# w_out with four consecutive rows on a partition, and layer one's weights taken from every fourth column of w_in

## The chip, the cores and the metric

The kernel runs on one core of one Trainium2 chip. The metric is the device time of one execution in microseconds (us). Executions of the kernel before agree within 0.6 us. Beside the times there is one execution recorded by the hardware profiler, with its own time; the rows and the trace that are read below come from that execution.

## What is computed

Sliding-window attention (a plain window of 32 keys for heads 0 to 3, a window of 32 keys at a distance of 4 for heads 4 to 7) is followed by a two-layer network with a SiLU between the layers. Only the second half is touched by the change:

```python
attn_out = _attn_ref(q, k, v)          # batch 8, heads 8, seq 576, head_dim 64
x = attn_out.transpose(0, 2, 1, 3).reshape(B * S, H * D)   # 4608 x 512
h = x @ w_in                           # w_in 512 x 2048
g = h * (1.0 / (1.0 + np.exp(-h)))
return (g @ w_out).astype(np.float32)  # w_out 2048 x 512
```

All inputs and the output are float32. The kernel works in float16 with float32 sums.

## The kernel before

**Batches and layers.** The outer loop runs over the 8 batches. For each batch, attention leaves its result transposed in `xT` (128 partitions, 4 pieces of 128 model columns, 576 positions). Layer one (`layer1`, from line 601; `layer1_part`, from line 618, for the two parts of batch 0) computes 16 groups `f` of 128 hidden units. A group takes 4 pieces `c` of the model dimension by 2 halves of the positions. Each of these 8 steps is a weight load of 128 x 128 elements of `w_in16` and a matmul over `xT` of 288 columns (line 606; 256 or 320 columns in batch 0, line 625). ScalarE then writes SiLU of the group to `gT[:, f, ...]` (lines 614 and 632). Layer two (`layer2_first` for batch 0, line 634; `layer2`, line 654) takes 128 positions of `gT[:, f]` as the stationary operand and `w_out16[:, f, :]`, 512 columns, as the moving one, and sums over the 16 groups (lines 642 and 666). `store` (lines 649 to 652) copies a sum to SBUF and sends it out on SP's queue.

**What a group is.** Hidden units are the sum index of layer two. Partition `p` of `gT[:, f]` and partition `p` of `w_out16[:, f]` must be the same hidden unit; which units make up a group is free, if all 2,048 are covered once.

**Loads of the weights.** Both weights are loaded in quarters of 512 hidden units, each with one DMA from GpSimd's queue, which also turns float32 into float16: `load_w_in(c)` at line 172 and `load_w_out(c)` at line 178. In `load_w_out` a partition gets four rows of a quarter, 128 rows apart.

**What sets the order.** Nothing is scheduled by a planner. Each engine runs its instructions in the order in which the program was written (`manual_schedule`, line 57), and the order around the layers is written by hand: `plan_of(b)` (line 690) gives, for each group `f` and for each step of layer two, the attention work of the next batches that is put in front of it. So TensorE's row is one fixed list in which stretches of layer-one matmuls, layer-two matmuls and small attention matmuls follow one another.

**GpSimd's queue.** It issues, in this order, the first batch's `q`, `k` and `v`, the four quarters of `w_in` (from 6.9 us), `load_qk(1)`, two quarters of `w_out`, `load_v(1)`, the other two quarters of `w_out` (lines 791 to 796), `load_qk(2)`, and the loads of the later batches. A DMA on this queue waits until the DMA eight places ahead of it has landed.

**PSUM.** The layers' sums `h` and `o` share two buffers (`big`); scores, transposes and attention results share four (`ps`).

Of the kernel before, what the change touches and what calls it, by code (L numbers as in the profile page):

```python
# [14 lines left out]
P = 128  # L15
# [12 lines left out]
def kernel(  # L28
# [44 lines left out]
    w_in16 = cpool.tile([P, MC, DFF], F16, name="w_in16")  # L73
# [96 lines left out]
    FC = DFF // 4  # L170

    def load_w_in(c):
# [2 lines left out]
            in_=moe_w_in[:, c * FC : (c + 1) * FC].rearrange("(c p) f -> p c f", p=P),  # L175
        )

    def load_w_out(c):
        nc.gpsimd.dma_start(
            out=w_out16[:, 4 * c : 4 * c + 4, :],  # L180
            in_=moe_w_out[c * FC : (c + 1) * FC, :].rearrange("(c p) m -> p c m", p=P),
        )


# [416 lines left out]
    def layer1(b, f):  # L601
        xT = state[b]["xT"]
        h = big.tile([P, 2, 512], F32, tag="big", name=f"h_{b}_{f}")
        for c in range(MC):
            for half in (0, 1):
                nc.tensor.matmul(  # L606
                    h[:, half, 0:HS],
                    w_in16[:, c, f * P : f * P + P],
                    xT[:, c, half * HS : half * HS + HS],
                    start=(c == 0),  # L610
                    stop=(c == MC - 1),
                )
        s0 = (b % 2) * S
        nc.scalar.activation(  # L614
            gT[:, f, s0 : s0 + S].rearrange("p (a c) -> p a c", a=2), h[:, :, 0:HS], AF.Silu
        )

    def layer1_part(f, part):

        xT = state[0]["xT"]  # L620
        c0, c1 = ((0, SA), (SA, S))[part]
        h = big.tile([P, 2, 512], F32, tag="big", name=f"h_0_{f}_{part}")
        for i in (0, 1):
            for c in range(MC):
                nc.tensor.matmul(  # L625
                    h[:, i, 0 : c1 - c0],
                    w_in16[:, c, (f + i) * P : (f + i + 1) * P],
                    xT[:, c, c0:c1],
                    start=(c == 0),
                    stop=(c == MC - 1),  # L630
                )
        nc.scalar.activation(gT[:, f : f + 2, c0:c1], h[:, :, 0 : c1 - c0], AF.Silu)  # L632
# [157 lines left out]

    load_qk(1)
    load_w_out(0)
    load_w_out(1)
    load_v(1)
    load_w_out(2)
    load_w_out(3)

# [28 lines left out]
    for b in range(B):  # L826
        plan = plan_of(b)
        if b == 0:
            for part in (0, 1):
                for f in range(0, NFF, 2):  # L830
                    plan(f - NFF * (1 - part))
                    plan(f - NFF * (1 - part) + 1)
                    layer1_part(f, part)
        else:
            for f in range(NFF):
                plan(f)
                layer1(b, f)
        if b == 0:
            layer2_first(plan)
        else:  # L840
            layer2(b, plan)
        for s in range(NFF, 3 * NFF):
            plan(s)
# [30 lines left out]
```

## Time and profile before

| | us |
|---|---|
| median of 3 runs | 332.45 |
| lowest, highest | 332.21, 332.79 |
| the profiled execution's own time | 331.63 |
| its span (first to last instruction) | 329.8 |

The span is what the rows below cover; the profiled execution's own time holds another 1.83 us around it. The median of the runs stands 0.82 us above the profiled execution.

The rows name engines as follows: PE is TensorE's matmul, PEld its weight load, DVE is VectorE, ACT ScalarE, POOL GpSimd and SP SyncE. A name like `h<-xT,w_in` gives the result and the operands. Matmuls are pipelined, so the duration of one (286 ns) is longer than the distance between two (122.5 ns).

| group | count | busy us | mean ns |
|---|---|---|---|
| layer one, matmul of 288 columns (L606) | 896 | 115.5 | 286 |
| layer one, weight load (L606) | 896 | 85.7 | 98 |
| layer one, batch 0, matmul (L625) | 128 | 17.8 | 293 (mean of two widths) |
| layer two, matmul (L666 and L642) | 592 | 130.4 | 373 and 379 |
| w_out, DMA issue on GpSimd (L179) | 4 | 3.05 | 753 (median) |

### The profile page before, as it was taken

How to read it: one execution, taken by the hardware profiler on the slowest of the kernel's cores; microseconds unless marked ns; L12 is line 12 of the kernel's file. 1: busy time of each engine (PE TensorE's matmuls, PEld its weight loads, DVE VectorE, ACT ScalarE, POOL GpSimd, SP SyncE). 2: the span in 40 equal slices, each digit the busy share in tenths (PEclk: the TensorE clock that was granted, in tenths of full speed). 3: DMA queues.
4: the chain of work that ended last, by engine and by line, in shares of the span. 5: the costliest groups of instructions: out<-in, count | busy, mean ns of one | idle time of the engine just before them, and what ended most of it. 6: DMA issues, size and time to landing. Idle time of an engine off the chain costs nothing.

```text
span 329.8 us, 11976 instructions
## 1 busy us (share of the span) xinstructions
PE 311.1 (94%) x5238; PEld 203.1 (62%) x5238; DVE 180.2 (55%) x377; ACT 214.8 (65%) x714; POOL 86.0 (26%) x144
## 2 busy tenths in 40 slices
PE   1679999999899999999999999999999999999996
PEld 1547764577545777467845677468755676467644
DVE  5778379745578744774557444774557442540011
ACT  2746669156599847985699357995699447916400
POOL 8743645544500560056004430042000000000000
PEclk9999999999999999999999999999999999999999
DMA  6999999999911975199404990175001100110022
GB/s 92 168 216 198 166 204 210 191 204 107 166 47 70 137 108 98 67 107 175 70 34 92 177 143 6 64 101 108 2 34 66 66 4 1 64 66 2 0 76 86
DMA packets 45141, 32.90 MB, mean 100 GB/s; under 512 B 21824, under 2 KB 39744, under 8 KB 45088
## 3 DMA queue, kind: packets, MB, share of 16 engines
q0 software_dynamic: 38752, 21.74, 48.5%
q1 hardware_dynamic: 6336, 10.39, 8.8%
q8 instruction: 41, 0.67, 0.9%
q14 instruction: 12, 0.10, 0.1%
HBM read 37.75 MB, written 9.44 MB: 143 GB/s over the span
## 4 chain that ended last, share of the span: by engine, by line
PE 79%; DMA 10%; DVE 4%; ACT 3%; POOL 2%; issue 2%; POOLq 0%
PE h L606 34%; PE o L666 31%; DMA n<-in_k_dram 4%; DMA vw<-in_v_dram 3%; PE t L260 3%; DMA n<-in_q_dram 3%; PE x L517 3%; PE pt L484 2%; ACT pe L459 2%; PE o L642 2%; PE s L318 1%; PE s L306 1%; DVE ms L415 1%; DVE pn L475 1%; DVE nm L431 1%
## 5 line engine op out<-in xcount | busy, mean ns | idle before, releaser
L614 ACT ACTIVATE gT<-h 128x576 f16<-128x576 f32 x112 | 72.8, 650 | 72.1 <-PE h L606 71.4
L606 PE MATMUL h<-xT,w_in 128*128 128x288 f16 x896 | 115.5, 286 | 0.8 <-issue 0.4
L666 PE MATMUL o<-w_out,gT 128*128 128x512 f16 (+1 forms) x528 | 115.6, 373 | 0.0
L606 PEld LDWEIGHTS <-w_in 128*128 128x128 f16 x896 | 85.7, 98 | 24.0 <-issue 1.3
L459 ACT ACTIVATE pe<-ms,nm 128x64 f32<-128x64 f32 x262 | 86.9, 334 | 0.1
L666 PEld LDWEIGHTS <-gT 128*128 128x128 f16 x528 | 50.0, 98 | 53.0
L651 DVE COPY ob<-o 128x512 f32<-128x512 f32 (+1 forms) x37 | 24.9, 674 | 53.6 <-PE o L666 53.1
L459 ACT ACTIVATION_READ_ACCUMULATOR pe<-ms,nm 128x1 f32 x262 | 49.2, 188 | 0.0
L415 DVE SCALAR_TENSOR_TENSOR ms<-s,mask 128x512 f32<-128x512 f32 x28 | 19.2, 686 | 39.1 <-PE ss L306 19.0
L123 POOL DMA_DIRECT2D vw<-in_v_dram x16 | 10.0, 632 | 84.8 <-PE x L517 84.3
L475 DVE TENSOR_TENSOR pn<-pe,r 128x640 f16<-128x640 f32 (+2 forms) x32 | 25.3, 792 | 1.1
L593 DVE CAST xT<-x 128x512 f16<-128x512 f32 x28 | 18.0, 686 | 11.7 <-PE xs L580 11.7
L431 DVE TENSOR_REDUCE nm<-ms 128x10 f32<-128x640 f32 (+1 forms) x28 | 22.0, 787 | 1.0
L102 POOL DMA_DIRECT2D n<-in_q_dram x28 | 16.4, 605 | 13.5 <-DMA w_in<-in_moe_w_in_dram 5.7
L102 POOL DMA_DIRECT2D n<-in_k_dram x28 | 16.5, 604 | 8.1 <-DMA w_in<-in_moe_w_in_dram 2.8
L492 DVE COPY ptT<-pt 128x640 f16<-128x640 f16 (+2 forms) x30 | 13.1, 472 | 9.9 <-PE pt L484 9.7
L625 PE MATMUL h<-xT,w_in 128*128 128x256 f16 (+1 forms) x128 | 17.8, 293 | 0.0
L632 ACT ACTIVATE gT<-h 128x512 f16<-128x512 f32 (+1 forms) x16 | 10.4, 650 | 8.1 <-PE h L625 7.9
L642 PE MATMUL o<-w_out,gT 128*128 128x512 f16 x64 | 14.8, 379 | 0.0
L625 PEld LDWEIGHTS <-w_in 128*128 128x128 f16 x128 | 12.3, 100 | 3.8 <-issue 0.5
L260 PEld LDWEIGHTS <-n 64*64 64x64 f16 (+1 forms) x840 | 10.0, 101 | 6.4 <-issue 5.1
L484 PE MATMUL pt<-ident,pn 128*128 128x128 f16 x152 | 12.2, 224 | 1.7 <-DVE pn L475 1.7
(84 smaller groups left out, 261.6 us busy)
## 6 DMA issues: line engine op xcount, KB each, us to landing
out_dram<-ob SPq DMA_DIRECT2D x35, 256.0 KB, 2.0
n<-in_k_dram POOLq DMA_DIRECT2D x28, 144.0 KB, 5.4
n<-in_q_dram POOLq DMA_DIRECT2D x28, 144.0 KB, 5.7
vw<-in_v_dram POOLq DMA_DIRECT2D x8, 288.0 KB, 7.0
vw<-in_v_dram POOLq DMA_DIRECT2D x16, 128.0 KB, 4.4
w_in<-in_moe_w_in_dram POOLq DMA_DIRECT2D x4, 512.0 KB, 12.5
w_out<-in_moe_w_out_dram POOLq DMA_DIRECT2D x4, 512.0 KB, 11.3
vw<-vw POOLq DMA_DIRECT2D x12, 128.0 KB, 3.7
```

The lines of the kernel that those rows point to most:

```text
L102: nc.gpsimd.dma_start(out=qk[b, z, which][i * HF : i * HF + UPS[z]].rearrange("p h u d -> p h (u d)"), in_=src[b, h : h + 2].rearrange("h ...
L260: nc.tensor.transpose(dst, w, ident[r, r])
L415: nc.vector.scalar_tensor_tensor(out=ms[:, 0:8].rearrange("p (n t) c -> p n (t c)", n=2), in0=s[hi].rearrange("p n t c -> p n (t c)"), sca ...
L431: nc.vector.tensor_reduce(out=nm[:, 0:w], in_=ms[:, 0:w], axis=AX.X, op=ALU.max, negate=True)
L459: nc.scalar.activation(pe[:, t, :], ms[:, t, :], AF.Exp, bias=nm[:, t : t + 1], accum_out=l[:, t : t + 1],)
L475: nc.vector.tensor_tensor(pn[:, 0:w], a["pe", z, hi][:, 0:w], r[:, 0:w, None].broadcast_to([P, w, KB]), ALU.mult)
L606: nc.tensor.matmul(h[:, half, 0:HS], w_in16[:, c, f * P : f * P + P], xT[:, c, half * HS : half * HS + HS], start=(c == 0), stop=(c == MC ...
L614: nc.scalar.activation(gT[:, f, s0 : s0 + S].rearrange("p (a c) -> p a c", a=2), h[:, :, 0:HS], AF.Silu)
L625: nc.tensor.matmul(h[:, i, 0 : c1 - c0], w_in16[:, c, (f + i) * P : (f + i + 1) * P], xT[:, c, c0:c1], start=(c == 0), stop=(c == MC - 1),)
L642: nc.tensor.matmul(o, gT[:, f, t * P : (t + 1) * P], w_out16[:, f, :], start=(f == 0), stop=(f == NFF - 1),)
L651: nc.vector.tensor_copy(ob, o)
L666: nc.tensor.matmul(o[:, 0, 0:m], gT[:, f, t * P : (t + 1) * P], w_out16[:, f, cols], start=(f == 0), stop=(f == NFF - 1),)
```

## The change

A quarter of `w_out` is laid out so that partition `p` holds the four consecutive rows `4p` to `4p + 3` of the quarter. What was four runs of 2 KB in HBM for a partition is one run of 8 KB, and in SBUF one run of 4 KB. Group `f = 4c + j` is now the hidden units `512c + 4n + j`, for `n` from 0 to 127. To match, layer one's weight load for group `f` takes every fourth column of the quarter, from column `j` on. In SBUF neighbouring elements of that load are 8 bytes apart, where they were 2 bytes apart. `w_in` itself is loaded as before.

```diff
+    def w_in_of(c, f):
+
+        return w_in16[:, c, f // 4 * FC : (f // 4 + 1) * FC].rearrange("p (n j) -> p j n", j=4)[:, f % 4]
+
     def load_w_out(c):
         nc.gpsimd.dma_start(
             out=w_out16[:, 4 * c : 4 * c + 4, :],
-            in_=moe_w_out[c * FC : (c + 1) * FC, :].rearrange("(c p) m -> p c m", p=P),
+            in_=moe_w_out[c * FC : (c + 1) * FC, :].rearrange("(p j) m -> p j m", p=P),
         )
...
-                    w_in16[:, c, f * P : f * P + P],
+                    w_in_of(c, f),
...
-                    w_in16[:, c, (f + i) * P : (f + i + 1) * P],
+                    w_in_of(c, f + i),
```

The order and the number of instructions on every engine are the same as before, and so are the semaphores that they wait for. In the compiled program each of layer one's 1,024 weight loads is still one instruction for 128 columns, read as four runs of 32 columns; the step between columns is four elements in place of one.

## The prediction

> **What bounds the kernel now.** I read the page's totals and slices first, then the stages, then TensorE's waits, then the rows of the two operands that change.
>
> ```profile
> PE 311.1 (94%) x5238; PEld 203.1 (62%) x5238; DVE 180.2 (55%) x377; ACT 214.8 (65%) x714; POOL 86.0 (26%) x144
> ...
> PE   1679999999899999999999999999999999999996
> ...
> PEclk9999999999999999999999999999999999999999
> DMA  6999999999911975199404990175001100110022
> ```
>
> TensorE is busy from the fourth slice (about 25 us) to the end, at a granted clock of 0.9 or more in every slice. The DMA engines are full in the first eleven slices, up to about 90 us, and loosely used afterwards.
>
> ```profile
> 25.50:36.60 11.10, 11.10 (x172) 8.89 (x171) 7.25 (x18) 6.58 (x10) 6.18 (x9) 1.00 1.11 180
> 36.60:48.00 11.40, 10.59 (x258) 7.67 (x258) 6.82 (x12) 7.17 (x11) 5.04 (x9) 1.00 1.45 191
> ...
> 160.00:200.00 40.00, 40.00 (x662) 25.80 (x660) 22.61 (x45) 28.57 (x100) 10.22 (x17) 1.00 0.55 94
> ```
>
> Here a row is a stage, its length, and the busy time of PE, PEld, DVE, ACT and POOL, then clock, DMA share and GB/s. In the stage from 36.6 to 48 us, where w_out's four quarters (issued at 31.6 to 39.4 us) mostly land, TensorE stands idle for 0.81 us, and from 160 to 200 us for nothing. The chain of waits gives DMA 10% of the span, but from 25 us on it runs past times in which TensorE worked; an earlier landing there shortens nothing by itself. What TensorE does wait for between 25 and 110 us is this:
>
> ```profile
> PE t L260 <- DVE ms L415: 0.9, 1, 0.9
> PE t L260 <- DMA vw<-in_v_dram: 0.8, 1, 0.8
> PE pt L484 <- DVE pn L475: 0.8, 1, 0.8
> PE h L606 <- issue: 0.4, 1, 0.4
> PE x L517 <- issue: 0.4, 1, 0.4
> PE h L606 <- DVE ob L651: 0.3, 1, 0.3
> ```
>
> That is 3.6 us in all. No row names w_out, and one names a DMA. So the time is TensorE's list of work, and the change counts by what it does to the distance between TensorE's instructions.
>
> **Part one: w_out's DMA.** The four issues take 752 to 798 ns on POOL, 3.05 us together. One of them after the change describes one run for a partition in place of four; the nearest cheap issue is a q load at about 600 ns, so the saving lies between 0 and 4 x 0.15 = 0.6 us of POOL. I take 0.3 us. POOL is busy for 26% of the span and TensorE waits for none of its own work, so that is 0 on the path.
>
> The transfers: before, 4 x 128 x 4 = 2,048 packets that write 1,024 B each. The trace's records of single packets on this queue have medians of 60 ns at 512 B, 98 ns at 1,024 B and 135 ns at 1,536 B, that is 75 ns per KB and some 23 ns that each packet costs whatever its size. A packet of 4,096 B would take 98 + 3 x 75 = 323 ns against 4 x 98 = 392 ns. Over 128 partitions and 16 engines that is 8 x 69 ns = 0.55 us for a quarter and **2.2 us of the DMA engines' time** for the four; it is 0 if the run is cut into packets of 1 KB again. It falls between 31.6 and some 50 us, where the queue is full, and GpSimd's next loads come as much earlier:
>
> ```profile
> POOL n L102 <- DMA w_out<-in_moe_w_out_dram: 2.8, 1, 2.8
> ...
> POOL w_out L179 <- DMA w_out<-in_moe_w_out_dram: 2.0, 1, 2.0
> ```
>
> These waits should shrink. Behind them stand q and k of batch 2, last issued at 53.5 us and landing some 6 us later, while TensorE first transposes them at 71.4 us: 10 us of cover. The shifts of v for batch 1 on SP's queue (43.5 to 47.4 us, landing in some 6 us) feed value matmuls at 58.9 us, again with 5 us to spare. So I take 0 on the path. The other side: a packet of 323 ns holds an engine longer than one of 98 ns, and what else passes the engines, instructions among them, waits behind it. TensorE's two waits named "issue" are 0.4 us each, so I bound this at 0.4 us either way.
>
> The 0.8 us named after v's DMA is at 45.02 us. I don't count it: the transposes that start there write a `ps` buffer, and VectorE's read of the scores that held one (L424, 44.79 us, 0.28 us long) ends at 45.07 us. VectorE had both scores of batch 1 to mask just before.
>
> **Part two: 1,024 weight loads with a step of four.** No load in the trace of before has a step, so its price has to be bounded. What a load in a row costs now:
>
> ```profile
> L606 PEld LDWEIGHTS <-w_in x896: 95/98/99, 66.6 to 309.0; 128*128 128x128 f16 x180
> L606 PE MATMUL h<-xT,w_in x896: 283/286/297, 67.4 to 309.1; 128*128 128x288 f16 x180
> ```
>
> The three durations are lowest, median and highest. The last batch's layer one, in the chain, is 128 matmuls in 15.68 us, one every 122.5 ns. In the single records a load starts about 2 ns after the matmul ahead of it, so it has some 120 ns before its own matmul is due (some 107 ns for the 256-column matmuls of batch 0, which follow one another every 109 ns). How little a packed load needs is in the transposes of attention:
>
> ```profile
> 179.56 0.77 PE L260 MATMUL t<-ident,n 48*128 48x48 f16 x48
> ...
> 189.38 0.67 PE L484 MATMUL pt<-ident,pn 128*128 128x128 f16 x9
> ```
>
> In the first row 48 matmuls, each behind its own load of 128 columns, take 0.77 us, of which the last one's own 0.18 us: one every 12.6 ns, two in turn on different partitions, so a load is done within 25 ns. In the second, whole loads of 128 by 128 pass every (0.67 - 0.22) / 8 = 56 ns. A load with a step would have to take over four times the 25 ns before a matmul in a row is late. **In the rows I take 0.**
>
> The place without cover is the start of a stretch. In the single records, layer one starts again after other work 42 times. In 27 of these the work ahead is on small tiles; there the load begins only when the small work is through, and the matmul starts 4 or 5 ns behind its own load. 21 of them are among the 896 of L606, and they are exactly the 21 that last 296 or 297 ns in place of 286 ns. So a load without cover shows as 11 ns now. If a step cost nothing the term is 0; if it doubled the load it is 27 x 11 ns = 0.3 us; if the load went at one column for each column that a transpose moves (the 56 ns of L484) it is 27 x (56 - 11) = 1.2 us. I take 0, as the load is the same instruction with as many columns and the packed row is its nearest; both ends stay in the range.
>
> One rule speaks for this and one against. The Trainium skill, "TensorE: Matmul & The Clock Gate", section "Weight-path perf modes — Fast Weight Load (FWL) and DoubleRow", says that the fast load is on for 128 weights that aren't FP32 and allows steps up to 1,024 elements; by it the sum stays 0, and the 25 ns above agree that the packed load is fast. The Trainium skill, "Advanced Engine Details and Errata", section "SBUF Cachelines", asks for at least two hits on a line of 16 bytes; a step of 8 bytes gives just two, where the packed load has eight. By the letter the sum stays 0 too, but with no margin; no trace here shows a load with a step.
>
> **Sum.** 331.63 us (the profiled execution) + 0 (w_out on the path) + 0 (loads in rows) + 0 (27 starts) = 331.6 us. The median of the runs is 0.82 us above that execution, so I forecast **332.4 us**, no change that a measurement of this kernel can tell: that takes about 0.2%, or 0.66 us. With the 0.4 us of issue either way and 0.3 us for the starts the forecast's own range is 331.8 to 333.1 us.
>
> **Rivals.**
> - *The step slows the load, and the starts pay (slower).* It decides once a load takes over some 11 + 660 / 27 = 35 ns: then 27 starts cost over 0.66 us. At 56 ns it gives 332.45 + 1.2 = 333.7 us; at twice that, 112 ns, 27 x 101 = 2.7 us, 7 starts behind a transpose with 54 ns of cover another 0.4 us, and 64 loads in the rows of 109 ns about 0.3 us: 335.8 us. Against it: each load still fetches 128 columns in one instruction. For it: it touches four times as many bytes' width of SBUF beside the moving operand's reads. If the two-hit rule were not enough, this is where it would show. Chance 0.20.
> - *The step slows the load past its cover (slower).* From 122 ns on every matmul of layer one is late: at 140 ns, 896 x 18 + 128 x 20 = 18.7 us, 351 us. A packed load would have to become over five times as long. Chance 0.08.
> - *TensorE was waiting for the queue after all (faster).* If the 0.8 us at 45.02 us is a DMA's and goes, 331.6 us; if the waits on VectorE around it shift with it, up to 3.6 us in all, 328.8 us. Against it is VectorE's row above. Chance 0.17.
> - *The DMA is cut as before.* Then part one is 0 and the time is the forecast's; it is inside the 0.55.
>
> **How the numbers follow.** Forecast 0.55, slower 0.20 + 0.08 = 0.28, faster 0.17. The range is 331.5 to 334.5 us: it leaves out the second rival (0.08), the upper part of the first (0.05) and the deeper part of the third (0.07).
>
> **What would show it.** Right: layer one's last stretch (128 matmuls) again in about 15.7 us, its matmuls at 286 ns with a highest of 297 ns, w_out landing sooner, fewer packets, POOL's waits for w_out shorter, and TensorE's waits before 110 us at about 3.6 us. Wrong by the first rival: a highest far over 297 ns or starts of stretches that come later. Wrong by the second: a distance over 122.5 ns in that last stretch, where no DMA is near. Wrong by the third: the wait at 45 us gone.

## The result, and the profile after

The change makes the kernel slower: 341.75 us, the median of 4 runs (340.07 to 342.94), against 332.55 us for the kernel before (332.21 to 332.79), a ratio of 1.027 with an interval from 1.023 to 1.032. A ratio compares only the fast executions of the two kernels; an execution over 1.5% above its kernel's fastest is left out. The prediction was 332.4 us, no change, with a range up to 334.5 us. The profiled execution took 341.59 us, with a span of 339.8 us where the one before had 329.8.

The page of the changed kernel, its totals and the slices of TensorE, of the granted clock and of the DMA engines (a slice is now 8.5 us long):

```profile
PE 314.9 (93%) x5238; PEld 219.7 (65%) x5238; DVE 180.8 (53%) x377; ACT 214.9 (63%) x714; POOL 85.2 (25%) x144
...
PE   2774999979979999999999999999999999999996
...
PEclk9996999999979999999999999999999999999999
DMA  7999999995631198219901983039001100110012
```

TensorE is busy 3.8 us longer, in a span that is 10.0 us longer. The fourth slice, in which it used to be full, has a 4, and the granted clock is low in the fourth and the twelfth slice, where it was 9 throughout. After that the rows look alike. The stages say the same in microseconds (columns as in the prediction: PE, PEld, DVE, ACT, POOL, clock, DMA share, GB/s):

```profile
25.50:36.60 11.10, 6.48 (x49) 4.91 (x53) 4.09 (x9) 3.08 (x5) 6.39 (x10) 0.69 1.12 198
...
160.00:200.00 40.00, 40.00 (x666) 27.88 (x665) 22.23 (x45) 28.54 (x100) 13.26 (x23) 1.00 0.59 102
```

From 25.5 to 36.6 us TensorE worked for 6.5 of 11.1 us at a mean clock of 0.69; before, it worked for all of it, at 1.00 by the row. (The trace of before holds no record of the clock ahead of 26.9 us, and the row shows 1.00 for that, too. Layer one's first six matmuls, ahead of that time, start 213 ns apart, and those behind it 109 ns: the clock was still at half for them.) What it waited for between 25 and 110 us (sum, times, longest):

```profile
PE h L629 <- DMA w_in<-in_moe_w_in_dram: 4.7, 1, 4.7
PE h L610 <- DVE ob L655: 2.1, 2, 1.7
PE t L264 <- DVE ms L419: 1.6, 2, 0.9
PE h L610 <- issue: 1.4, 1, 1.4
PE pt L488 <- DVE pn L479: 0.8, 1, 0.8
```

The first row is new: layer one waits for w_in, a transfer that the change doesn't touch. TensorE's list at that place, before and then after (start, length, group; in brackets the idle time ahead of it):

```profile
25.69 3.40 PE L625 MATMUL h<-xT,w_in 128*128 128x256 f16 x24
28.92 0.50 PE L484 MATMUL pt<-ident,pn 128*128 128x128 f16 x6
```

```profile
25.17 0.28 PE L629 MATMUL h<-xT,w_in 128*128 128x256 f16 x1
30.12 5.07 PE L629 MATMUL h<-xT,w_in 128*128 128x256 f16 x23 [4.67 <-DMA w_in<-in_moe_w_in_dram]
34.98 0.70 PE L488 MATMUL pt<-ident,pn 128*128 128x128 f16 x6
```

One matmul of layer one runs; the second one's weight load waits until 30 us. In the program the reason is plain, and the semaphores in the traces' records of the loads say the same: in the kernel before, the first load of each quarter waits for that quarter of w_in. In the changed kernel **the second load of all waits for the other three quarters at once**, and the last of these was issued at 14.1 us and landed 15.9 us later. The sentence ahead of the prediction, that the semaphores waited for are the same as before, is wrong, and so is what rests on it.

Where the 10.0 us come up, by the start of the same matmul in both traces:

| start of | before | after | difference |
|---|---|---|---|
| layer one, first matmul | 25.69 | 25.17 | -0.52 |
| transposes behind its first 24 matmuls | 28.92 | 34.98 | 6.06 |
| layer two, first matmul | 47.81 | 54.09 | 6.28 |
| layer one of batch 1, 33rd matmul | 72.13 | 79.71 | 7.58 |
| layer two of batch 1, first matmul | 89.06 | 97.88 | 8.82 |
| layer one of the last batch | 293.57 | 303.56 | 9.99 |

The wait and the slow clock behind it make 6.6 us (6.06 + 0.52, as layer one had started 0.52 us earlier). Then 1.3 us come, net, where TensorE waits for VectorE, which itself waits for a store to land:

```profile
75.18 0.69 DVE L655 COPY ob<-o 128x512 f32<-128x512 f32 x1 [2.16 <-DMA out_dram<-ob]
```

Another 1.2 us come by a wait at 96 us that the profile names "issue", and about 1 us by the half clock behind that one. Over the 200 us that follow, the difference hardly grows. "Issue" says only that the profile shows nothing that TensorE waited for. Here it fits a wait for instructions: a packet of 16 KB on the queue that the page calls "instruction" lands at 96.00 us, 1.4 us before the wait ends, and in the traces of all 14 kernels each of TensorE's waits of that name from 20 to 100 us, if it lasts 0.2 us or more, ends 1.2 to 1.6 us after such a packet has landed. Below these are called waits for instructions.

### The profile page after: what moved, and what is told of

Read it like the earlier page. It is cut to its first block, busy times and chain, and to the rows that moved or that the text cites. A ratio compares the mean times of both kernels' runs of the same rounds, so it can differ in the third digit from the quotient of the medians.

```text
span 339.8 us, 11977 instructions
## 1 busy us (share of the span) xinstructions
PE 314.9 (93%) x5238; PEld 219.7 (65%) x5238; DVE 180.8 (53%) x377; ACT 214.9 (63%) x714; POOL 85.2 (25%) x144
## 2 busy tenths in 40 slices
DMA packets 43605, 32.90 MB, mean 97 GB/s; under 512 B 21824, under 2 KB 37696, under 8 KB 43552
## 4 chain that ended last, share of the span: by engine, by line
PE 81%; DMA 8%; DVE 4%; ACT 2%; POOL 2%; issue 1%; DVEq 0%; POOLq 0%
PE h L610 33%; PE o L670 30%; PE h L629 5%; DMA w_in<-in_moe_w_in_dram 5%; PE t L264 3%; PE x L521 2%; PE pt L488 2%; ACT pe L463 2%; PE o L646 2%; DMA out_dram<-ob 1%; DMA n<-in_q_dram 1%; PE s L322 1%; PE s L310 1%; DVE ms L419 1%; DVE nm L435 1%
## 5 line engine op out<-in xcount | busy, mean ns | idle before, releaser
L610 PEld LDWEIGHTS <-w_in 128*128 128x128 f16 x896 | 99.6, 114 | 13.9 <-issue 4.2
L629 PE MATMUL h<-xT,w_in 128*128 128x256 f16 (+1 forms) x128 | 19.9, 313 | 4.7 <-DMA w_in<-in_moe_w_in_dram 4.7
L629 PEld LDWEIGHTS <-w_in 128*128 128x128 f16 x128 | 14.5, 121 | 8.3 <-issue 5.5
L636 ACT ACTIVATE gT<-h 128x512 f16<-128x512 f32 (+1 forms) x16 | 10.4, 651 | 14.9 <-PE h L629 14.8
L646 PE MATMUL o<-w_out,gT 128*128 128x512 f16 x64 | 14.8, 379 | 0.0
```

The lines of the kernel that those rows point to most:

```text
L610: nc.tensor.matmul(h[:, half, 0:HS], w_in_of(c, f), xT[:, c, half * HS : half * HS + HS], start=(c == 0), stop=(c == MC - 1),)
L629: nc.tensor.matmul(h[:, i, 0 : c1 - c0], w_in_of(c, f + i), xT[:, c, c0:c1], start=(c == 0), stop=(c == MC - 1),)
L646: nc.tensor.matmul(o, gT[:, f, t * P : (t + 1) * P], w_out16[:, f, :], start=(f == 0), stop=(f == NFF - 1),)
```

## The experiments

Theory A: the loss is that one wait and what follows from it. Theory B: the wait is only part of it, and w_out's larger packets or the step in the loads cost the rest. In these runs the kernel before took from 330 to 338 us, more spread than beside the result, so the ratios have wider intervals, and some are not told apart; the 0.6 us within which its first executions agreed does not hold here. The expectations in microseconds are for a kernel before of 332.5 us and are compared by their ratios.

**Each load waits for its own quarter again.** A quarter is made one interval of a partition; steps and w_out's layout stay.

```diff
-    w_in16 = cpool.tile([P, MC, DFF], F16, name="w_in16")
+    w_in16 = cpool.tile([P, 4, MC, DFF // 4], F16, name="w_in16")
...
-        return w_in16[:, c, f // 4 * FC : (f // 4 + 1) * FC].rearrange("p (n j) -> p j n", j=4)[:, f % 4]
+        return w_in16[:, f // 4, c].rearrange("p (n j) -> p j n", j=4)[:, f % 4]
...
-            out=w_in16[:, :, c * FC : (c + 1) * FC],
+            out=w_in16[:, c],
```

> The changed kernel with one thing undone: w_in16 is laid out with the quarter outermost, so that a quarter is one interval of a partition and a weight load with a step waits for its own quarter alone, as before the change. Steps of four and w_out's new layout stay. Theory A (the loss is the second load's wait for all four quarters, and what follows from that wait): the wait of 4.7 us and the half clock behind it go, 332.2 to 333.0 us; what stays is the starts of stretches, whose first matmul lasts 313 ns in place of 296 ns, 27 x 17 ns = 0.5 us, against w_out's earlier landing. Theory B (the wait is only part of it; the larger packets of w_out hold up the stores and the instructions, which made TensorE wait 1.8 us and 1.4 us more at 74 and 96 us): 335 to 336 us, since 10.0 - 6.3 = 3.7 us remain.

Measured: 333.65 us, ratio 1.0026 (0.9985 to 1.0066). The wait for w_in is gone from the list of waits, and in the stage that took the first loss TensorE works for 10.5 of the 11.1 us, at a clock of 1.00:

```profile
25.50:36.60 11.10, 10.47 (x170) 9.24 (x169) 7.66 (x19) 6.65 (x11) 6.28 (x10) 1.00 1.13 197
```

Most of the loss went with the wait, while the step and the new w_out stayed. B's 335 us and more, a ratio from 1.0075 on, is out. A's 332.2 to 333.0 us, ratios of 0.999 to 1.0015, lies inside the interval, though the median lies above it; some tenths of a per cent may remain.

**Its control:** the kernel before with the same layout of w_in16.

> The control for the one above: the kernel before with w_in16's quarter outermost, packed loads, w_out as before. The semaphores waited for are those of before. Both theories: 332.2 to 332.8 us, no difference; a difference here would be the layout's own (w_in lands in one run of 4 KB for a partition).

Measured: 331.45 us, ratio 0.9982 (0.9943 to 1.0021): no difference, as both theories had it.

**The wait alone.** In the kernel before, the second load, and no other, is given a step:

```diff
-                    w_in16[:, c, (f + i) * P : (f + i + 1) * P],
+                    w_in16[:, 1, 0:FC].rearrange("p (n j) -> p j n", j=4)[:, 0] if (f, i, part, c) == (0, 0, 0, 1) else w_in16[:, c, (f + i) * P : (f + i + 1) * P],
```

> The kernel before with the wait alone: of the 1,024 weight loads of layer one only the second (group 0, second piece of the model dimension, first part of batch 0) is read with a step of four, from columns that belong to another group, so that group 0 of 256 positions is summed with one wrong block of weights. That one load now waits for all four quarters of w_in, as in the changed kernel. w_out as before. Theory A: the whole loss is there, 340 to 342 us. Theory B: only the wait and its half clock, 332.5 + 6.3 = 338.5 to 339 us, with no longer waits for stores and instructions at 74 and 96 us.

Measured: 340.61 us, ratio 1.0246 (1.0187 to 1.0304), beside the change's 1.0274 (1.0229 to 1.0319). TensorE's list there:

```profile
25.31 0.27 PE L625 MATMUL h<-xT,w_in 128*128 128x256 f16 x1
30.30 5.07 PE L625 MATMUL h<-xT,w_in 128*128 128x256 f16 x23 [4.72 <-DMA w_in<-in_moe_w_in_dram]
```

(The profiled execution is the longest of this kernel's six, 344.08 us.) One load in 1,024, with w_out untouched and all other loads packed, brings the same wait, the same slow 23 matmuls and a loss that can't be told from the whole one. Theory A's number was 340 to 342 us. Theory B's 338.5 to 339 us, ratios of 1.018 to 1.0195, lies at the lower end of the interval and is not wholly out by the time, but the longer waits for a store and for instructions, which B did not expect here, stand in the trace (1.8 and 2.2 us).

**w_out's layout alone.**

```diff
-            in_=moe_w_out[c * FC : (c + 1) * FC, :].rearrange("(c p) m -> p c m", p=P),
+            in_=moe_w_out[c * FC : (c + 1) * FC, :].rearrange("(p j) m -> p j m", p=P),
```

> The kernel before with w_out's new layout alone: packed loads of w_in as before, so that groups of hidden units and rows of w_out do not belong together and the output is another sum of the same products' size. Theory A: w_out lands some 2 us earlier and TensorE waits for nothing less, 332.0 to 332.7 us. Theory B: the larger packets cost TensorE waits for stores and instructions, 335 to 336 us.

Measured: 333.46 us, ratio 1.0050 (1.0007 to 1.0092). A gain is ruled out. A's 332.0 to 332.7 us (ratios up to 1.0006) end just below the interval; B's 335 us (1.0075) lies above the median and inside the interval. So the new packets may cost from nothing to 0.9%: the interval ends just above no change, and the profiled execution (span 330.1 us against 329.8) shows no new wait.

**The step alone**, with the quarter outermost and w_out as before.

> Weight loads with a step of four alone, each waiting for its own quarter (w_in16 with the quarter outermost), w_out's layout as before, so that groups of hidden units and rows of w_out don't belong together and the output is another sum. Theory A: the step costs the 27 starts without cover some 17 ns each, 0.5 us, ratio to before 1.001 to 1.002; distances in rows of matmuls stay 122.5 ns. Rival C (the step has a cost that the starts don't show, such as readers of SBUF that slow each other): a ratio over 1.004, with longer distances or longer instructions on other engines.

Measured: 334.06 us, ratio 1.0009 (0.9959 to 1.0060). No loss to be seen, which fits A's 0.5 us, but the interval is too wide to measure it and reaches past rival C's 1.004. The rows of matmuls stayed 122.5 ns apart, where C had longer distances.

**TensorE kept at work through the wait.**

```diff
-    keep_busy(2)
+    keep_busy(24)
     load_qk(2)
```

> The changed kernel with 22 more matmuls of 512 columns on the identity ahead of layer one, whose result nobody reads: TensorE works through most of the 4.7 us that it would stand in the second weight load's wait. The wait itself stays where it was. Theory A with the clock as a part of its own: the matmuls behind the wait run at the full clock (24 in 3.4 us in place of 5.1 us), so 1.7 to 2 us of the loss go: a ratio to before of about 1.022 where the change has 1.027. Rival D (the half clock has another cause than standing still, or hides behind another wait): no difference to the change, 1.027.

Measured: 340.55 us, ratio 1.0254 (1.0193 to 1.0315): between the two expectations and telling neither from the other. The stage itself is clear:

```profile
25.50:36.60 11.10, 11.03 (x118) 7.95 (x117) 4.93 (x11) 3.73 (x6) 6.19 (x10) 1.00 1.13 199
```

The clock is 1.00 where the change had 0.69, and the transposes behind the first 24 matmuls start at 33.00 us in place of 34.98. Layer one's first 24 matmuls take 3.02 us, less than the 3.40 us of before, as all of them now run at the whole clock. So standing still was what cost the clock, and the clock was worth 2.0 us at that place. But layer two starts at 54.00 us, where the change had 54.09: TensorE waited 1.9 us for instructions in between, and the gain was gone.

**Six output buffers in place of three**, in the changed kernel.

```diff
-    o32 = ctx.enter_context(tc.tile_pool(name="o32", bufs=3))
+    o32 = ctx.enter_context(tc.tile_pool(name="o32", bufs=6))
```

> The changed kernel with six output buffers in SBUF in place of three (o32). In the changed kernel VectorE waited 2.2 us for a store to land before it could write the fourth output tile of batch 0, and TensorE 1.7 us for VectorE; in the kernel before TensorE's wait there was 0.3 us. Theory A with the stores as a part of the loss: that wait goes, a ratio to before of 1.021 to 1.023 in place of 1.027. Rival (the wait for stores stands beside another that ends as late): still 1.027.

Measured: 338.76 us, ratio 1.0178 (1.0127 to 1.0230). Among the waits, the first is still there and the second has fallen from 2.1 to 0.4 us:

```profile
PE h L629 <- DMA w_in<-in_moe_w_in_dram: 4.6, 1, 4.6
...
PE h L610 <- DVE ob L655: 0.4, 1, 0.4
```

The rival's 1.027 is out; A's 1.021 to 1.023 lies in the upper part of the interval. So the wait for a store was part of the time. How much of the loss it is, is another matter: six buffers may help the kernel before, too (0.9958, below), and beside that one the change with six buffers is still some 2.2% slower (1.0178 / 0.9958). The wait isn't the work of w_out's packets alone: the profile of the kernel with the wait alone, which has w_out as before, shows it too (1.8 us in all), and that of the step alone, with no delay at all, 3.2 us, both in long executions of their kernels (344.08 and 336.65 us). It comes and goes, and how much of it the delay brings is not settled.

**The change without the wait and with six buffers**, the best that the findings point to:

> The change with w_in16's quarter outermost (each load waits for its own quarter) and six output buffers: what the findings so far point to as the best kernel that keeps w_out's new layout. Theory A: the store waits, 0.3 to 2.8 us in the profiles, go: a ratio of 0.993 to 0.999. Rival: the instruction waits of 1 to 2 us and what follows them stay and cover it, 1.000 to 1.003.

Measured: 334.16 us, ratio 1.0022 (0.9981 to 1.0064). Its waits for instructions (1.9 us at the longest) and a clock of 0.994 stand in that execution. The ratio is the rival's; the interval still takes in the top of A's.

**The kernel before with six buffers:**

> The control for the two above: the kernel before with six output buffers. Theory A: 0.994 to 0.999, as its own store wait is 0.3 us in the profiled execution and up to 2 us in others. Rival: 1.000.

Measured: 330.69 us, ratio 0.9958 (0.9913 to 1.0003). It may be a little faster than before; the interval just takes in no change. No kernel here beats the one before for certain.

Beside this control the change without the wait is 0.6% slower (1.0022 / 0.9958), though the two intervals overlap. Other runs lean the same way: with w_out's new layout and no wait for w_in the ratios are 1.0026, 1.0050 and, with a step of eight below, 1.0100 (0.4% of it the loads); with the old layout and no wait they are 0.9982, 1.0009 and 0.9958. So w_out's new layout may cost some 0.5%, 1 to 2 us, beside what the wait costs. No run here settles it or shows how.

**The size of the step.** Three kernels with other steps, the rows of w_out arranged to match.

```diff
-        return w_in16[:, c, f // 4 * FC : (f // 4 + 1) * FC].rearrange("p (n j) -> p j n", j=4)[:, f % 4]
+        return w_in16[:, c, f // 8 * 2 * FC : (f // 8 + 1) * 2 * FC].rearrange("p (n j) -> p j n", j=8)[:, f % 8]
...
```

> One size changed: eight consecutive rows of a half of w_out on a partition, loaded in four transfers of the change's size, and weight loads with a step of eight elements (16 bytes) in a half of w_in. A load waits for two quarters of w_in at a time. Looked at for the load's duration (98 ns packed, 113 ns with a step of four) and for what it does to starts and rows. Theory L (the cost goes by the 16-byte lines that the load touches: 4 for each run of 32 columns packed, 16 with a step of four, 32 from a step of eight on): 98 + 15 x 28/12 = 133 ns, starts at 296 + 35 = 331 ns, rows still 122.5 ns apart. Theory S (it goes by the bytes spanned): 98 + 15 x 7/3 = 133 ns here too. Theory H (below two hits on a line the price jumps): over 160 ns, and rows of matmuls further apart than 122.5 ns. Time: between before and the change, since q0 and q1 land before q3.

```diff
+        return w_in16[:, c].rearrange("p (n j) -> p j n", j=16)[:, f]
...
```

> As the one above with sixteen consecutive rows of all of w_out on a partition, and weight loads with a step of sixteen elements (32 bytes) over all of w_in; the first load waits for all four quarters, as in the change. Theory L: the load lasts 133 ns as with a step of eight. Theory S: 98 + 15 x 15/3 = 173 ns, past the 164 ns or so from which a row of matmuls would be late. Theory H: as with a step of eight. Time: that of the change (ratio 1.027) plus 27 x 20 ns = 0.5 us by L, plus 896 x 9 ns = 8 us by S.

```diff
+        return w_in16[:, c, f // 2 * 2 * P : (f // 2 + 1) * 2 * P].rearrange("p (n j) -> p j n", j=2)[:, f % 2]
...
```

> One size changed, for the load's duration alone: two consecutive rows on a partition, weight loads with a step of two elements (4 bytes), waits as in the changed kernel. Measured so far: 98 ns packed, 113 ns with a step of four, 143 ns with eight, 144 ns with sixteen. If the cost goes by the 16-byte lines that a load touches (4, 16, 32, 32 for each run of 32 columns), a step of two (8 lines) gives 98 + 15 x 4/12 = 103 ns. If it is free up to some number of elements on a line (four here), 98 ns. If any step costs the same first price, 113 ns.

The loads of layer one, lowest, median and highest duration in ns, in the kernels with a step of two, of four (the changed kernel), of eight and of sixteen; the packed load's row is in the prediction (95/98/99):

```profile
L610 PEld LDWEIGHTS <-w_in x896: 96/98/152, 72.4 to 320.5; 128*128 128x128 f16 x180
```

```profile
L610 PEld LDWEIGHTS <-w_in x896: 110/113/133, 72.3 to 319.0; 128*128 128x128 f16 x180
```

```profile
L610 PEld LDWEIGHTS <-w_in x896: 140/143/171, 66.9 to 311.3; 128*128 128x128 f16 x180
```

```profile
L610 PEld LDWEIGHTS <-w_in x896: 140/144/170, 73.2 to 318.0; 128*128 128x128 f16 x180
```

A step of two is free, four costs 15 ns, eight costs 45 ns, and sixteen no more than eight. As far as these five points tell, the cost follows how many of a load's elements share 16 bytes (eight, four, two, one, one) and not how far the load reaches: theory S's 173 ns is out. It isn't a price for each line of 16 bytes either, as that had 103 ns for a step of two and 133 ns for eight; theory H had over 160 ns and wider rows. In the single records the matmuls at uncovered starts last 297 ns (step of two), 313 ns (four), 344 ns (eight) and 342 ns (sixteen), against 296 ns packed, while rows of matmuls stay 122.5 ns apart in all of them.

The times: step of eight 335.77 us, ratio 1.0100 (1.0047 to 1.0152), with no wait for w_in, since the first load waits for two quarters only; of that, 27 starts x 48 ns = 1.3 us or 0.4% are the loads, and the other 0.6% is not accounted for. Step of sixteen 342.46 us in two runs, ratio 1.0299 (1.0181 to 1.0416), with a wait of 5.1 us at the first load; the profile names it after a load of k, but that weight load needs all four quarters of w_in, and the last of them lands just before 30.3 us. Step of two 343.1 us in one run, with the wait of 4.7 us. **Even a step that costs the load nothing has the whole loss, if the wait is there.**

## Why the prediction was wrong, point by point

- **The step that failed** is the sum, "331.63 us (the profiled execution) + 0 (w_out on the path) + 0 (loads in rows) + 0 (27 starts)". It has no term for a wait, because the waits had been taken to be the same. Part two asked only how long a load with a step takes, and the rivals only how far it could slow the rows. The missing term is 4.7 us of wait, 1.9 us of half clock behind it (6.6 us, or 2.0% of 331.6), and what came later, some 4 us in the profiled execution, which differs between executions. How much of that the delay brings, and how much w_out's new layout, stays open.
- *TensorE's list is what counts.* Right, and the reason why the wait is paid in full: nothing in an in-order list covers it. The profile before even had the number that would have priced it: w_in's transfers, issued from 12.6 to 14.8 us, land 10.8 to 15.6 us later, so a load at 25.7 us that needed all of them would wait to about 30 us.
- *w_out's DMA.* The sizes were right. Four packets of 98 ns have become one; in the records 512 packets of 4,096 B have a median of 322 ns (estimated 323 ns), and the page counts 43,605 packets in place of 45,141, 1,536 fewer. The landing is 9.3 us at the median in place of 11.3. The issue is cheaper than I bounded it: four of 539 to 612 ns, some 2.25 us in place of 3.05, so 0.8 us of POOL and not 0.6 at most. That none of it shortens the time was right: w_out alone gained nothing (1.0050). Whether the bound of 0.4 us on what the larger packets can cost was right, the runs don't tell; 1 to 2 us are possible.
- *Loads in rows, 0.* Right: the last batch's layer one takes the 15.68 us of before in the chain of waits, though each load lasts 113 ns in place of 98:

```profile
303.72 15.68 PE h L610 x128
```

- *The 27 starts.* The mechanism was right and the value I took (0) was not: 313 ns in place of 296 ns, 27 x 17 ns = 0.5 us, inside the bounds of 0 and 1.2 us.
- *The rivals.* None had this mechanism. The first and the second rested on the load's duration, which is not what cost the time; that the measured ratio lies on their side is no support for them. The second's price, "From 122 ns on every matmul of layer one is late", must not be read by the durations in the records: loads recorded at 143 and 144 ns (steps of eight and sixteen) left the rows at 122.5 ns. The packed load is recorded at 98 ns and passes every 56 ns in the transposes, so by this estimate some 42 ns of a record don't hold up the row. That would put the limit for a record at 122 + 42 = 164 ns, the figure in the expectation for a step of sixteen. The third is out: TensorE's wait at the same place (51.3 us in the changed kernel) is still 0.7 us, and is named after VectorE.
- *The clock.* The prediction reads a granted clock of 0.9 or more in every slice off the page, but a 9 also stands where the trace holds no record of it. Layer one's first six matmuls ran at half.
- *The two rules of the skill.* The fast load does work with a step, as the trace agrees for steps of two (98 ns). The two-hit rule (the Trainium skill, "Advanced Engine Details and Errata", section "SBUF Cachelines") asks for at least two hits on a line of 16 bytes; here two are not quite enough: two elements on 16 bytes cost 15 ns, and four are free.

Open: why the program gives the second load that wait. It comes with steps of two and of four in the old layout of w_in16 and is gone with the quarter outermost; with a step of eight the loads wait only for the two quarters that they read. No run here shows the rule behind it. Open too is why the delay was followed by more waits for stores and for instructions, since these differ between executions of one kernel.

## What to carry to other kernels

When an access pattern changes, read the waits of the program's instructions one by one, before and after, above all for the first users of each load; equal numbers and order of instructions say nothing of them. Price a new wait from rows that are already there: when the transfer lands, against when its first user stood. And if a packed tile gets a strided reader, lay it out so that what one transfer writes is one interval of a partition.

## What the runs showed that I had not expected

Standing still for 4.7 us halved TensorE's clock for what came next: the matmuls behind the wait took 5.07 us for 23, where 24 had taken 3.40 with the first six of them at half clock, and 3.02 when TensorE was kept at work. The mean clock was 0.69 from 25.5 to 36.6 us, which is 0.31 x 11.1 / 0.5 = 6.9 us at half; the trace's own record has half from 28.6 to 35.4 us, so it fell 3.1 us after TensorE's last matmul. The Trainium skill, "TensorE: Matmul & The Clock Gate", section "Why this matters for your kernels", warns of gaps over some 3 us between matmuls, which this agrees with. But the clock was at half again from 96.9 to 100.3 us, where no gap was longer than 1.4 us (0.9 us and 1.4 us, with 1.5 us of small transposes and six matmuls between them); there the measurement shows more than that warning says.

The clock's row can also miss it. In the kernel with a step of sixteen the trace's first record of the clock stands at 36.1 us, and the row says 1.00 for the whole stage, while its matmuls crawl as in the changed kernel:

```profile
30.40 5.31 PE L629 MATMUL h<-xT,w_in 128*128 128x256 f16 x24 [5.06 <-DMA n<-in_k_dram]
...
25.50:36.60 11.10, 6.20 (x35) 5.13 (x36) 3.78 (x9) 3.06 (x4) 6.41 (x10) 1.00 1.11 193
```

That is one start in 213 ns. So the distance between matmuls of one shape is the surer sign of the clock.
